# A fused attention, routing and expert kernel on one core: staged q and k halves written in place, narrow expert products, two output tiles begun together, more keep-warm matmuls

## The chip, the cores and the metric

One core of one Trainium2 chip runs the whole program. The metric is the device time of one execution in microseconds (us). Three executions before the change took 561.7, 564.54 and 566.77 us, median 564.54. The profiled execution, from which every row below comes, took 564.97 us, with a span of 563.3 us from its first to its last instruction.

## The reference, cut to what matters

```python
def _attn_ref(q, k, v, tau):            # 2 batches, 8 heads, 576 tokens, 64 per head
    scores = scale * np.matmul(q, k.transpose(0, 1, 3, 2))
    thresh = np.max(scores, axis=-1, keepdims=True) - tau
    scores = np.where(scores >= thresh, scores, -1000000000.0)
    ...softmax over the last axis...
    return np.matmul(attn, v)
def _moe_ref(x, w_gate, w1, w2, capacity):   # 1152 tokens, 512 wide, 8 experts, 1024 inside
    expert_idx = np.argmax(x @ w_gate, axis=1)
    ...each token to its one expert: out = gate * (relu(x @ w1[e]) @ w2[e])
def _moe2_ref(x, w_gate, w_val, w_out):      # 1536 inside, weights in float64
    g = x @ w_gate
    return (g / (1 + exp(-g)) * (x @ w_val)) @ w_out
```

The three run one after the other. Sums are kept near float32 precision: most operands are split in a high part rounded to the matmul's fp32r format and a low rest, and a product is made of hi*hi, hi*lo and lo*hi.

## The kernel before, in words

**Attention** (lines 308 to 963) takes the heads in four pairs (`hp` 0 to 3) and each pair in nine units (`st` 0 to 8): 128 query rows of one batch for both heads `j`, and as the ninth the 64 tail rows of both batches. A unit computes scores (`emit_qk`, L597: high and low part of q as stationary operand, one after the other, against `KP`, which holds k's high part in one half of the partitions and its low part in the other), the row maximum (L607), exp (L620), the mask (L631), the transposes of the previous unit (L653, copied out at L657), and some of a queue of other work: products with v (`pv_tasks`, L675 for the four main blocks of 128 keys, L678 for the 64 tail keys, where each head uses its own half of the partitions), the turning of the next pair's q and k, and the product with the router's weights (L709). The order on TensorE, VectorE (DVE), ScalarE (ACT) and GpSimd (POOL) is the order of the program text; SyncE (SP) issues nearly all DMAs, one after the other.

**Staging of the next pair** (`stage_tasks`, lines 493 to 574) is queued at unit `TST`, 4, and taken up from the next unit on, two tasks a unit; from unit `UST`, 5, these tasks go ahead of v products. A task turns 512 columns of k or q (`main`) or the tails of both, ACT copies the result, POOL writes the rounded part (L508) and the rest (L510) of all 128 partitions to a scratch tile, and SP copies from there by DMA to the places that `emit_qk` reads: 4 DMAs for each k main (L537), 4 for each q main (L540), 4 for k's tails (L559), and 8 for q's tails (L568, `qtails`, at unit `QST`, 1, of the pair itself). Per pair these are 28 DMAs. The order of tasks is k of batch 0, q of batch 0, tails, k of batch 1, q of batch 1. The first unit of the next pair needs the first three.

**Routing** (lines 966 to 1126) sorts tokens by expert in a chain of small DVE operations with a few matmuls between, with `keep_warm` matmuls on a zero tile (L775) behind three of its steps (`WA`). It ends in a branch on the load of the experts; the trace runs the branch `FAST`, in which the experts, sorted by load, have windows of 128, 128, 128, 144, 176, 192, 224 and 224 tokens. Behind the branch the first 128 gathered rows are scaled (L1181), turned (L1187), copied in two parts (L1193, L1194), and used by the first expert (L1267).

**Experts.** Those of width W above 128 go through `expert` (L1349). For each of 8 blocks `f` of the inner width, four partial products give `ps_h`; for each of 4 blocks `m` of the output, eight partial products over `f` give `ps_y`. A partial product (`mm_win`) is two matmuls: the weights' high part against both parts of the window side by side (2W columns, L1231), and their low part against the high part (W columns, L1232). `total` then adds the two halves: an ACT copy (L1240) and a DVE add (L1241). The relu is split by ACT (L1357) and DVE (L1358), one block behind. Between them the same two engines turn raw weights into pieces (L210, L288), and behind the first output block DVE cuts the next expert's window (`window`, L1226, L1227). `expert` issues output blocks one after the other, each followed by its way out to `yT` (L1240, L1241, L1405, L1406).

**The last layer** follows (L1447 on): TensorE products for gate and value, then for the output, with float64 weights converted by ACT and DVE meanwhile.

Of the kernel before, what the change touches and what calls it, by code (L numbers as in the profile page):

```python
# [10 lines left out]
F32 = mybir.dt.float32  # L11
# [11 lines left out]
def attention_moe_swiglu_kernel(  # L23
# [55 lines left out]
    WA = (4,9,12,0)  # L79
# [6 lines left out]
    TST = 4  # L86
    QST = 1
    FB = 1800
# [5 lines left out]
    UST = 5  # L94
# [222 lines left out]
    idw = ld.tile([128, KD, 128 + 2 * NE], F32, name="idw")  # L317

    def load_qkv(hp):
# [3 lines left out]
        for nm, (src, nb) in srcs.items():  # L323
            if hp and nm != "v":
                r[nm] = ld.tile([128, B, C4, 2, D], F32, tag=nm, name=nm, bufs=nb)
            else:
                r[nm] = ld.tile([128, B, 2, C4, D], F32, tag=nm, name=nm, bufs=nb)
            r[nm + "t"] = ld.tile([128, 2, D], F32, tag=nm + "t", name=nm + "t", bufs=nb)

        def main(nm, b, eng):  # L330
            if hp and nm != "v":
                for h in range(2):
                    eng.dma_start(r[nm][:, b, :, h],
                                  srcs[nm][0][b, h0 + h, 0:SM, :].rearrange("(p c) d -> p c d", c=C4))
# [4 lines left out]
        def tail(nm, eng):  # L339
            src = srcs[nm][0]  # L340
            for i in range(2):
# [6 lines left out]
                eng.dma_start(r[nm + "t"][i * ST:(i + 1) * ST], src_t)  # L348
# [7 lines left out]
        for b in range(B):  # L356
            main("v", b, nc.sync)
        tail("v", nc.sync)
# [42 lines left out]
    QT = [ld.tile([128, 2, 2 * 128], F32R, name=f"qt{j}") for j in range(2)]  # L401
    QTH, QTL = [[QT[j][:, w] for j in range(2)] for w in range(2)]
    traw = ld.tile([128, 2, 128], F32, name="traw")
    thl = ld.tile([128, 2, 2, 128], F32R, name="thl")
    qhl = [ld.tile([128, 2, B * SM], F32R, name=f"qhl{j}") for j in range(2)]
    ready = set()

    def tr_qk_tasks(hp):
# [6 lines left out]
        def ensure(j):  # L415
            if (hp, j) not in KP:
                KP[hp, j] = qk.tile([128, B, S], F32R, tag=f"kp{j}", name=f"kp{j}")
                QH[hp, j], QL[hp, j] = qhl[j][:, 0], qhl[j][:, 1]
                if hp % 2 == 0:
                    QH[hp, j], QL[hp, j] = ring[3 + j][:, 0], ring[3 + j][:, 1]  # L420
# [14 lines left out]
        def qmain(b, j, w):  # L435
            def f():
                ps = mp.tile([128, 512], F32R, tag="m", name="ps_q")
                tr(ps, [fl(raw[hp]["qh" if w == 0 else "ql"][:, b, j, c]) for c in range(C4)])
                dst = (QH, QL)[w][hp, j][:, b * SM:(b + 1) * SM]
# [53 lines left out]
    def stage_tasks(hp):  # L493
        kx, qx = ring[1], ring[0]
# [3 lines left out]
        def ensure():  # L498
            if (hp, 0) in KP:
                return  # L500
            for j in range(2):
                KP[hp, j] = qk.tile([128, B, S], F32R, tag=f"kp{j}", name=f"kp{j}")
                QH[hp, j], QL[hp, j] = qhl[j][:, 0], qhl[j][:, 1]
                if hp % 2 == 0:
                    QH[hp, j], QL[hp, j] = ring[3 + j][:, 0], ring[3 + j][:, 1]

        def parts(dst, src):
            nc.gpsimd.tensor_scalar(out=dst[0], in0=src, scalar1=1.0, scalar2=1.0,  # L508
                                    op0=ALU.mult, op1=ALU.mult)
            nc.gpsimd.tensor_tensor(out=dst[1], in0=src, in1=f32(dst[0]), op=ALU.subtract)  # L510
# [7 lines left out]
        def main(nm, b):  # L518
            def f():
# [4 lines left out]
                x, dst = (kx, sraw[:, 1, cs]) if nm == "k" else (qx, sraw[:, 0, cs])  # L524

                def ev():
# [19 lines left out]
        def tails():  # L546
# [3 lines left out]
            def ev():  # L550
# [3 lines left out]
                parts([thl[:, i] for i in range(2)], traw)  # L554
                for j in range(2):
                    o = 0 if j else SM
                    frm = slice(j * D, (j + 1) * D)
                    for i in range(2):
                        nc.sync.dma_start(  # L559
                            f32(KP[hp, j][i * D:(i + 1) * D, :, o:o + ST]),  # L560
# [996 lines left out]
```

## Time and profile before

| | |
|---|---|
| three executions | 561.7, 564.54, 566.77 us |
| profiled execution | 564.97 us, span 563.3 us |
| mean granted TensorE clock | 0.986 of full |
| attention, first score product to last | 9.8 to about 171 us |
| routing and branch | about 172 to 187 us |
| experts | 187 to 332 us |
| last layer | 332 to 559 us |

Read it by stretches: a share of busy time over the whole span mixes stages that wait for different things. In the rows below a time in front is the start in us from the span's beginning. A clock of 1.00 is 2.4 GHz and 0.50 is 1.2 GHz.

### The profile page before, as it was taken

To read this page: it belongs to the slowest core of one execution; us is meant where nothing else is said; L and a number is where in the kernel's file an instruction comes from. 1 tells how busy PE (TensorE), PEld (TensorE's weight loads), DVE (VectorE), ACT (ScalarE), POOL (GpSimd) and SP (SyncE) were. 2 spreads that over 40 slices of the span, in tenths; PEclk is the share of its full clock that TensorE was granted. 3 is DMA by queue.
4 is the path that set the end of the run, shared out by engine and by line. 5 is a ranking of instruction groups with operands and counts; after the bars stand their busy time and mean duration, and the time that the engine had idled before them with its cause. 6 is when DMAs were issued, how large, how long until landed. Compare 5 with 4: busy or idle time off the path is not lost. (4 is left out here: it accounts for less than half of the span.)

```text
span 563.3 us, 9844 instructions
## 1 busy us (share of the span) xinstructions
PE 536.4 (95%) x3600; PEld 481.0 (85%) x3602; DVE 409.7 (73%) x825; ACT 295.2 (52%) x573; POOL 85.4 (15%) x145
## 2 busy tenths in 40 slices
PE   7999988999997799999999999999999999999996
PEld 6787866877773799998998889999999999888884
DVE  5988876888876399989988977888896748722220
ACT  4977664676651399877866743334332333332321
POOL 6541050055452500000000000000000000011101
PEclk8999998999999799999999999999999999999999
DMA  7557467457301888977666442442341300000001
GB/s 185 173 150 171 118 143 172 110 140 205 116 29 35 313 289 281 328 224 232 224 219 223 151 149 81 145 149 83 143 149 76 112 40 1 0 38 37 20 38 42
DMA packets 67895, 77.94 MB, mean 138 GB/s; under 512 B 25216, under 2 KB 43136, under 8 KB 67840
## 3 DMA queue, kind: packets, MB, share of 16 engines
q1 hardware_dynamic: 66256, 72.52, 42.4%
q0 software_dynamic: 1440, 4.72, 2.2%
q8 instruction: 30, 0.49, 0.3%
q14 instruction: 25, 0.20, 0.1%
q10 hardware_dynamic: 144, 0.00, 0.0%
HBM read 61.89 MB, written 4.72 MB: 118 GB/s over the span
## 5 line engine op out<-in xcount | busy, mean ns | idle before, releaser
L1460 PE MATMUL pgv<-yT,ring 128*128 128x384 f32 x828 | 145.1, 337 | 0.0
L1460 PEld LDWEIGHTS pgv<-yT,ring 128*128 128x128 f32 x828 | 144.9, 188 | 0.0
L210 ACT CAST ring<-raw 128x1024 fp32r<-128x1024 f32 x57 | 60.8, 1066 | 51.2 <-DVE raw L238 49.5
L657 ACT COPY pT<-ps_pt 128x512 f32<-128x512 f32 (+1 forms) x108 | 52.3, 486 | 41.6 <-PE ps_pt L653 41.6
L607 DVE TENSOR_REDUCE nm<-s 128x1 f32<-128x576 f32 x72 | 54.4, 755 | 17.2 <-PE s L597 17.1
L631 DVE SCALAR_TENSOR_TENSOR e<-s,th,e 128x576 f32<-128x576 f32 x72 | 58.7, 816 | 6.2 <-ACT e L620 4.9
L1513 POOL DMA_INDIRECT out_dram<-ob,ids x9 | 8.7, 972 | 358.9 <-ACT ob L1512 351.7
L620 ACT ACTIVATE e<-s,nm 128x576 f32<-128x576 f32 x72 | 54.3, 754 | 2.2 <-DVE nm L607 1.8
L288 DVE TENSOR_TENSOR ring<-raw,ring 128x1024 fp32r<-128x1024 f32 x44 | 53.3, 1218 | 0.0
L1231 PE MATMUL ps_y<-h,ring 128*128 128x448 f32 (+3 forms) x160 | 48.8, 370 | 3.6 <-DVE h L1358 3.4
L214 DVE TENSOR_TENSOR hs<-h,hs 128x768 fp32r<-128x768 f32 x18 | 17.2, 958 | 48.1 <-ACT hs L210 48.1
L653 PE MATMUL ps_pt<-ident,e 128*128 128x128 f32 x324 | 47.9, 276 | 0.0
L1231 PE MATMUL ps_h<-xw,ring 128*128 128x448 f32 (+3 forms) x160 | 46.4, 362 | 0.0
L1508 PE MATMUL po<-ring,hs 128*128 128x512 f32 x108 | 42.0, 389 | 0.0
L1507 PE MATMUL po<-ring,hs 128*128 128x512 f32 x108 | 42.0, 389 | 0.0
L1509 PE MATMUL po<-ring,hs 128*128 128x512 f32 x108 | 42.0, 389 | 0.0
L1232 PE MATMUL ps_y<-h,ring 128*128 128x224 f32 (+3 forms) x160 | 40.0, 250 | 0.0
L1232 PE MATMUL ps_h<-xw,ring 128*128 128x224 f32 (+3 forms) x160 | 40.0, 250 | 0.0
L675 PE MATMUL ps_pv<-pT,v 128*64 128x256 f32 (+2 forms) x400 | 39.9, 331 | 0.0
L653 PEld LDWEIGHTS ps_pt<-ident,e 128*128 128x128 f32 x324 | 39.7, 142 | 0.2 <-issue 0.2
L1231 PEld LDWEIGHTS ps_y<-h,ring 128*128 128x128 f32 x160 | 30.0, 188 | 8.3 <-DVE h L1358 7.4
L1480 ACT ACTIVATE sg<-pgv 128x384 f32<-128x384 f32 x36 | 17.5, 486 | 28.4 <-PE pgv L1460 18.9
(224 smaller groups left out, 975.9 us busy)
## 6 DMA issues: line engine op xcount, KB each, us to landing
raw<-in_moe_w_dram SPq DMA_DIRECT2D x25, 1024.0 KB, 5.1
rawx<-in_moe_w_dram SPq DMA_DIRECT2D x7, 1024.0 KB, 5.9
raw<-in_moe_w_gate_dram SPq DMA_DIRECT2D x6, 1024.0 KB, 5.0
qhl<-ring SPq DMA_DIRECT2D x16, 256.0 KB, 4.4
raw<-in_moe_w_out_dram SPq DMA_DIRECT2D x4, 1024.0 KB, 4.9
kp<-ring SPq DMA_DIRECT2D x24, 128.0 KB, 2.3
rawx<-in_moe_w_val_dram SPq DMA_DIRECT2D x3, 1024.0 KB, 5.0
raw<-in_moe_w_val_dram SPq DMA_DIRECT2D x3, 1024.0 KB, 5.0
```

The source lines that it names most:

```text
L210: nc.scalar.copy(dst, src)
L288: lo_eng.tensor_tensor(out=lo_, in0=src, in1=f32(hi_), op=ALU.subtract)
L607: nc.vector.tensor_reduce(out=nm_t[u][:, j:j + 1], in_=s_t[i][:, :, 0:SH], axis=AX.XY, op=ALU.max, negate=True)
L620: nc.scalar.activation(out=e_t[u][:, j].rearrange("p (a s) -> p a s", a=2), in_=s_t[i][:, :, 0:SH], func=ACTF.Exp, bias=nm_t[u][:, j:j + 1 ...
L631: nc.vector.scalar_tensor_tensor(out=ev, in0=s_t.pop(i)[:, :, 0:SH], scalar=th_t[u][:, j:j + 1], in1=ev, op0=ALU.is_ge, op1=ALU.mult, accu ...
L653: nc.tensor.transpose(ps[:, c * 128:(c + 1) * 128], ef[:, (c0 + c) * 128:(c0 + c + 1) * 128], ident)
L657: return lambda: nc.scalar.copy(pT[g][:, c0:c0 + m, o:o + 128], ps[:, 0:m * 128].rearrange("p (c t) -> p c t", c=m))
L1231: mm(ps[:, 0:2 * W], ws(wp, 0), x[:, 0:2 * W], start=first, stop=False)
L1232: mm(ps[:, 0:W], ws(wp, 1), x[:, 0:W], start=False, stop=last)
L1460: mm(ps[:, 0:TH], (gw, vw)[w][:, i, kk, fl * 128:(fl + 1) * 128], yT[:, x, kk, th * TH:(th + 1) * TH], start=i + x + kk == 0, stop=i == 1 ...
L1507: mm(po, hs[:, 0, fl], ws[:, 0, sl], start=f == 0, stop=False)
L1508: mm(po, hs[:, 0, fl], ws[:, 1, sl], start=False, stop=False)
```

## The change

Attention. The four raw loads of q and k per pair become one DMA per tensor and batch. v's tail rows get a tile of their own per parity of the pair, zeroed once at the start by two DVE memsets; each head's 64 rows stand in its own half of the partitions with zeros in the other half, so that the tail product runs over all 128 partitions. Loads of v for pairs 2 and 3 move from unit 0 to unit 5 (`VST`). Staging is queued at unit 3 and goes first from unit 4. POOL now writes rounded part and rest separately for each half of the partitions, in place where the part already lies in the right half, and SP copies only the other half: 2 DMAs for each main, 2 for k's tails, 2 for q's tails (which POOL rounds in place first), 12 per pair in all. The tails come second in the order of tasks.

Routing and branch. Sixteen `keep_warm` matmuls of 512 columns follow the branch, four more follow the first transposes. A memset of the end of `xsT` moves from DVE to POOL. `late_consts` moves from unit 5 to unit 11. Nine small tiles share one buffer.

Experts. `mm_win` uses two matmuls up to 2W = 400, three of W columns above (the two experts of 224), and `total` then adds nothing. For the experts above 128, the first two output blocks are begun together: six partial products of block 0, six of block 1, then the last two of each.

```diff
-    WA = (4,9,12,0)
+    WA = (4,9,12,16,4)
-    TST = 4
+    TST = 3
+    VST = 5
-    UST = 5
+    UST = 4
...
+    vtail = [ld.tile([128, B, 2, D], F32, name=f"vtail{i}") for i in range(2)]
...
-                for h in range(2):
-                    eng.dma_start(r[nm][:, b, :, h], ...)
+                eng.dma_start(r[nm][:, b], ...)
...
-                eng.dma_start(r[nm + "t"][i * ST:(i + 1) * ST], src_t)
+                dst = r[nm + "t"][i * ST:(i + 1) * ST]
+                eng.dma_start(dst[:, :, i] if nm == "v" else dst, src_t)
...
+        if hp < 2:
+            values()
+        else:
+            vlate[hp] = values
...
-                    parts([x[:, i, cs] for i in range(2)], dst)
-                    for j in range(2):
-                        for i in range(2):
-                            to, frm = slice(i * D, (i + 1) * D), slice(j * D, (j + 1) * D)
-                            if nm == "k":
-                                o = ST if j else 0
-                                nc.sync.dma_start(f32(KP[hp, j][to, b, o:o + SM]), f32(x[frm, i, cs]))
-                            else:
-                                t = ring[3 + j] if hp % 2 == 0 else qhl[j]
-                                nc.sync.dma_start(f32(t[to, :, cs]), f32(x[frm, :, cs]))
+                    if nm == "k":
+                        k0, k1 = [KP[hp, j][:, b, o:o + SM] for j, o in ((0, 0), (1, ST))]
+                        x = kx[:, cs]
+                        rounded(k0[lo_], dst[lo_])
+                        rest_of(x[lo_], dst[lo_], k0[lo_])
+                        nc.sync.dma_start(f32(k0[up]), f32(x[lo_]))
+                        rounded(x[up], dst[up])
+                        rest_of(k1[up], dst[up], x[up])
+                        nc.sync.dma_start(f32(k1[lo_]), f32(x[up]))
+                    else:
+                        for j, frm, to in ((0, lo_, up), (1, up, lo_)):
+                            t = by_batch(ring[3 + j] if hp % 2 == 0 else qhl[j])[:, b]
+                            rounded(t[frm, 0:SM], dst[frm])
+                            rest_of(t[frm, SM:2 * SM], dst[frm], t[frm, 0:SM])
+                            nc.sync.dma_start(f32(t[to]), f32(t[frm]))
...
+                q4 = QT[j][:, :].rearrange("p (y t) -> p y t", t=ST)[:, 0:10:3]
+                x = thl[:, :, :].rearrange("p w (b t) -> p (w b) t", b=B)
+                rounded(q4[frm], f32(x[frm]))
+                nc.sync.dma_start(f32(q4[to]), f32(x[frm]))
...
-        return [main("k", 0), main("q", 0), tails, main("k", 1), main("q", 1)], qtails
+        return [main("k", 0), tails, main("q", 0), main("k", 1), main("q", 1)], qtails
...
-                        mm(ps[j * D:(j + 1) * D, o:o + w], r["vt"][j * ST:(j + 1) * ST, bb, :],
-                           p[j * ST:(j + 1) * ST, C4, o:o + w], start=False, stop=True)
+                        mm(ps[j * D:(j + 1) * D, o:o + w], r["vt"][:, bb, j, :],
+                           p[:, C4, o:o + w], start=False, stop=True)
...
-        for ev in [sort_tile(t) for t in range(NS0)]:
+        evs = [sort_tile(t) for t in range(NS0)]
+        keep_warm(ps8, WA[4])
+        for ev in evs:
             ev()
...
-        V.memset(xsT[:, :, NT:], 0.0)
+        nc.gpsimd.memset(xsT[:, :, NT:], 0.0)
...
-            if 2 * W <= 512:
+            if 2 * W <= 400:
...
-            if 2 * W > 512:
+            if 2 * W > 400:
                 return ps[:, 0:W]
...
+            head, tail_ = range(KF - 2), range(KF - 2, KF)
...
+                    if m == 0:
+                        products(0, head)
+                        products(1, head)
+                        products(0, tail_)
+                        products(1, tail_)
+                    elif m > 1:
+                        products(m, range(KF))
```

## Rows read from the trace of the kernel before

**Rows 1.** The page, part 1: busy us of each engine, share of the span.

```profile
PE 536.4 (95%) x3600; PEld 481.0 (85%) x3602; DVE 409.7 (73%) x825; ACT 295.2 (52%) x573; POOL 85.4 (15%) x145
```

**Rows 2.** Waits, whole span: who waited for whom, us in total, times, longest.

```profile
DVE nm L607 <- PE s L597: 17.1, 22, 3.3
...
PE ps_y L1231 <- DVE h L1358: 3.4, 5, 1.1
PE s L597 <- DMA kp<-thl: 3.4, 2, 3.1
```

**Rows 3.** Windows: stretch, us, busy PE, PEld, DVE, ACT, POOL, clock, DMA share, GB/s.

```profile
86.50:89.90 3.40, 3.40 (x17) 2.97 (x17) 2.31 (x4) 1.71 (x4) 0.00 (x0) 0.50 0.55 136
...
185.50:192.30 6.80, 5.99 (x28) 5.59 (x27) 2.83 (x6) 2.22 (x3) 5.25 (x6) 0.50 1.02 396
```

**Rows 4.** Timeline of SP's queue, 60 to 90 us: start, us, issues merged.

```profile
62.58 6.15 SPq L568 DMA_DIRECT2D qt<-thl  x8
...
70.72 3.11 SPq L537 DMA_DIRECT2D kp<-ring  x4
...
79.73 3.23 SPq L559 DMA_DIRECT2D kp<-thl  x4
```

**Rows 5.** Timeline of POOL, 58 to 92 us: start, us.

```profile
72.01 0.61 POOL L508 TENSOR_SCALAR ring<-raw 128x512 fp32r<-128x512 f32 x1
72.71 1.29 POOL L510 TENSOR_TENSOR ring<-raw,ring 128x512 fp32r<-128x512 f32 x1
```

**Rows 6.** Groups by line: busy us, mean ns.

```profile
L678 PE MATMUL ps_pv<-pT,vt 64*64 64x256 f32 (+2 forms) x100 | 13.3, 342 | 0.0
```

**Rows 7.** Timelines of PE, main and tail products with v, 48 to 53 us.

```profile
48.01 0.39 PE L675 MATMUL ps_pv<-pT,v 128*64 128x256 f32 x2
48.32 0.43 PE L678 MATMUL ps_pv<-pT,vt 64*64 64x256 f32 x2
...
48.59 0.38 PE L678 MATMUL ps_pv<-pT,vt 64*64 64x256 f32 x2
...
51.15 1.95 PE L675 MATMUL ps_pv<-pT,v 128*64 128x256 f32 x16
```

**Rows 8.** Timeline of PE, 178 to 198 us, around the branch.

```profile
179.37 2.75 PE L775 MATMUL ps_w<-dummy 128*128 128x512 bf16 x11
185.39 1.02 PE L1187 MATMUL ps_g<-ident,raw 128*128 128x128 f32 x4 [3.26 <-DVE raw L1181]
187.21 5.38 PE L1267 MATMUL ps_h<-ring,xw 128*128 128x256 f32 x24 [0.81 <-issue]
...
194.88 1.68 PE L1267 MATMUL ps_h<-ring,xw 128*128 128x256 f32 x12
```

**Rows 9.** Windows, columns as in rows 3: inner and output stretches of three experts.

```profile
249.81:258.57 8.76, 8.76 (x66) 8.76 (x65) 7.83 (x17) 6.95 (x17) 0.00 (x0) 1.00 0.66 210
258.57:269.13 10.56, 9.45 (x67) 8.82 (x65) 9.55 (x20) 7.00 (x16) 0.00 (x0) 1.00 0.74 252
...
298.77:309.68 10.91, 10.78 (x66) 9.56 (x65) 9.54 (x17) 6.84 (x15) 0.00 (x0) 1.00 0.68 226
309.68:319.71 10.03, 10.03 (x66) 9.57 (x65) 9.42 (x18) 8.46 (x19) 0.00 (x0) 1.00 0.66 212
319.71:332.02 12.31, 11.29 (x66) 9.56 (x65) 11.16 (x24) 5.76 (x14) 0.00 (x0) 1.00 0.27 83
```

**Rows 10.** Timeline of weight loads (PEld) in an expert of 224.

```profile
306.14 0.19 PEld L1231 LDWEIGHTS ps_y<-h,ring 128*128 128x128 f32 x1
306.25 0.19 PEld L1232 LDWEIGHTS ps_y<-h,ring 128*128 128x128 f32 x1
306.45 0.19 PEld L1231 LDWEIGHTS ps_y<-h,ring 128*128 128x128 f32 x1
```

**Rows 11.** Timelines of PE and of DVE, output stretch of the expert of 176.

```profile
261.22 0.43 PE L1231 MATMUL ps_y<-h,ring 128*128 128x352 f32 x1 [1.11 <-DVE h L1358]
...
263.22 0.33 DVE L1241 TENSOR_TENSOR a<-a,ps_y 128x176 f32<-128x176 f32 x1
```

More of the change, by code (lines that the diff above doesn't have):

```diff
@@ L355, in load_qkv, with values @@
         tail("q", nc.sync)
-        for b in range(B):
-            main("v", b, nc.sync)
-        tail("v", nc.sync)
+        def values():
+            for b in range(B):
+                main("v", b, nc.sync)
+            tail("v", nc.sync)
+        if hp < 2:
+            values()
+        else:
+            vlate[hp] = values
+    vlate = {}
     def prep_tasks(hp, pick):
@@ L400, in attention_moe_swiglu_kernel, with by_batch, q_pair @@
     QH, QL, KP = {}, {}, {}
-    QT = [ld.tile([128, 2, 2 * 128], F32R, name=f"qt{j}") for j in range(2)]
-    QTH, QTL = [[QT[j][:, w] for j in range(2)] for w in range(2)]
+    QT = [ld.tile([128, 5 * 128], F32R, name=f"qt{j}") for j in range(2)]
+    QTH, QTL = [[QT[j][:, w * 384:w * 384 + 256] for j in range(2)] for w in range(2)]
     traw = ld.tile([128, 2, 128], F32, name="traw")
-    thl = ld.tile([128, 2, 2, 128], F32R, name="thl")
+    thl = ld.tile([128, 2, 128], F32R, name="thl")
+    kth = ld.tile([128, 128], F32R, name="kth")
     qhl = [ld.tile([128, 2, B * SM], F32R, name=f"qhl{j}") for j in range(2)]
     ready = set()
+    def by_batch(t):
+        return t[:, :, :].rearrange("p w n -> p (w n)").rearrange("p (b n) -> p b n", b=B)
+    def q_pair(hp, j):
+        t = by_batch(ring[3 + j] if hp % 2 == 0 else qhl[j])
+        return [t[:, :, w * SM:(w + 1) * SM] for w in range(2)]
     def tr_qk_tasks(hp):
@@ L417, in ensure @@
                 KP[hp, j] = qk.tile([128, B, S], F32R, tag=f"kp{j}", name=f"kp{j}")
-                QH[hp, j], QL[hp, j] = qhl[j][:, 0], qhl[j][:, 1]
-                if hp % 2 == 0:
-                    QH[hp, j], QL[hp, j] = ring[3 + j][:, 0], ring[3 + j][:, 1]
+                QH[hp, j], QL[hp, j] = q_pair(hp, j)
         def kmain(b, j):
@@ L493, in stage_tasks @@
     def stage_tasks(hp):
-        kx, qx = ring[1], ring[0]
+        kx = ring[1][:, 0]
         sraw = raw_buf[2][:, :].rearrange("p (i n) -> p i n", i=2)
@@ L502, in ensure, with rounded, rest_of @@
                 KP[hp, j] = qk.tile([128, B, S], F32R, tag=f"kp{j}", name=f"kp{j}")
[L503 to L508, printed above, removed]
+                QH[hp, j], QL[hp, j] = q_pair(hp, j)
+        def rounded(dst, src):
+            nc.gpsimd.tensor_scalar(out=dst, in0=src, scalar1=1.0, scalar2=1.0,
                                     op0=ALU.mult, op1=ALU.mult)
-            nc.gpsimd.tensor_tensor(out=dst[1], in0=src, in1=f32(dst[0]), op=ALU.subtract)
+        def rest_of(dst, src, hi):
+            nc.gpsimd.tensor_tensor(out=dst, in0=src, in1=f32(hi), op=ALU.subtract)
         def turn(blocks, name):
@@ L523, in f @@
                 cs = slice(b * SM, (b + 1) * SM)
-                x, dst = (kx, sraw[:, 1, cs]) if nm == "k" else (qx, sraw[:, 0, cs])
+                dst = sraw[:, 1 if nm == "k" else 0, cs]
                 def ev():
@@ L778, in attention_moe_swiglu_kernel @@
     keep_warm(mp, WARM0, 128)
+    for vz in vtail:
+        nc.vector.memset(vz, 0.0)
     nc.scalar.dma_start(tau_sb, tau.partition_broadcast(128))
@@ L938, in attention_moe_swiglu_kernel @@
             qtails()
+        if live and st == VST and hp + 1 in vlate:
+            assert not any(g[0] < hp for _, _, g in pvq)
+            vlate.pop(hp + 1)()
     assert not trq
@@ L1386, in expert, with products @@
                         next_piece()
+            pys = {}
+            def products(m, fs):
+                if fs[0] == 0:
+                    ps = ps8.tile([128, 512], F32, tag="m", name="ps_y")
+                    pys[m] = ps, pieces.pop(("w2", e, m))[:, :, :].rearrange(
+                        "p i (k f) -> p i k f", k=KF)
+                ps, wv = pys[m]
+                for f in fs:
+                    mm_win(W, ps, wv, lambda w, i: w[:, i, f], hs[f], f == 0, f == KF - 1)
+            head, tail_ = range(KF - 2), range(KF - 2, KF)
             for m in range(KD):
-                ps = ps8.tile([128, 512], F32, tag="m", name="ps_y")
                 if e in halves:
+                    ps = ps8.tile([128, 512], F32, tag="m", name="ps_y")
                     for f in range(KF):
@@ L1395, in expert @@
                 else:
-                    wp = pieces.pop(("w2", e, m))
-                    wv = wp[:, :, :].rearrange("p i (k f) -> p i k f", k=KF)
-                    for f in range(KF):
-                        mm_win(W, ps, wv, lambda w, i: w[:, i, f], hs[f], f == 0, f == KF - 1)
+                    if m == 0:
[5 more added lines that the diff above has]
+                        products(m, range(KF))
+                    ps = pys[m][0]
                 if e == 0:
```

50 lines of the change are left out of this document (27 added, 23 removed).

## The prediction

> **What bounds the kernel now.** The first part of the page [rows 1] gives TensorE 95% busy, so only TensorE's own time counts: what its work takes, the gaps in it, and the stretches in which its clock is half. The view of waits [rows 2] gives the gaps by releaser, the windows [rows 3] the two long stretches at 0.50 that end a gap, and the timelines and windows of stretches [rows 4 to 11] the price of each step. DVE is 73% busy over the span, which hides that it sets the pace in single stretches: 9.55 of 10.56 us in one output stretch [rows 9]. The sum is made against the profiled execution, 564.97 us; the median of the runs is 0.43 us lower. One per cent, 5.6 us, is about what a measurement of this kernel can tell from no change.
>
> **Staging of q and k.** Now: TensorE waits for k's tails (`kp<-thl`) 3.4 us in two places, 3.1 of it before the second pair [rows 2], and runs the 3.40 us behind that at 0.50 [rows 3], which costs half of them, 1.7 us. The wait's last link is SP's queue: SP works through 28 issues per pair one by one, 6.15/8 = 0.77 us each for `qtails`, 3.11/4 = 0.78 for a k main, 3.23/4 = 0.81 for k's tails, and these last four end at 79.73 + 3.23 = 82.96 us [rows 4], with the landing behind that. After: 12 issues, some 9.5 us instead of 22, and half the bytes; the tails stand second, not third, and the tasks start a unit earlier (about 4 us). The raw loads' halves merge, which takes two issues per tensor and batch to one; moving v's loads of the later pairs to unit 5 puts at most some 8 issues (6.3 us) into SP's queue among the staged copies, but behind the tails' and k's copies of batch 0 and, at the worst, ahead of q's. The added price is POOL's: a main takes 0.61 + 1.29 = 1.9 us on 128 partitions [rows 5]; on 64 partitions an instruction takes at least half of that (sum 1.9, nothing lost) and, if only the columns count, as much (3.8 us). I take the upper end, since the two instructions move the same 512 columns. The chain on POOL before the next pair's first unit is then k 3.8, tails some 2.3 (by the same rows, with 128 columns for four instructions of each kind: (0.61 + 1.29) × 128/512 × 4 = 1.9, and starts), q 3.8, together 9.9 us. Begun one unit earlier than the 72.01 us of now, less the tasks that stand ahead, at about 66, it ends near 76; two issues and a landing later, near 81, q stands ready, against 82.5 when TensorE comes. The slack of 1.5 us is small, and a later boundary has the same. So the wait vanishes: −3.4 − 1.7 = **−5.1**; bounds 0 (a new wait of the same size) and −5.1. `qtails` gets POOL work of a quarter of a main at unit 1 and is needed at unit 8: hidden. The memsets of v's tail tiles lie on DVE in the start, ahead of the first scores, where the engines wait for loads; without that cover, two instructions of some 0.3 us. The memset moved to POOL (15% busy) and `late_consts` at unit 11: nothing, as both have tens of us until the first reader.
>
> **v's tail products.** 100 of them, now 64*64 [rows 6]. Two main products in a row start 1.95 − 0.39 = 1.56 us over seven steps of pairs apart, 0.22 per pair; from a main to a tail pair it is 48.32 − 48.01 = 0.31, and from the first tail pair to the next 0.27 [rows 7]. So a change of shape costs (0.31 + 0.27 − 2 × 0.22) = 0.14 us. With 128 rows there is none. The trace has 19 changes into the tail form and 12 back into the main form: 31 × 0.14 = 4.3 us. Attention is at TensorE's pace in the last three pairs (DVE waits for scores 17.1 us in 22 places [rows 2]) and at DVE's in the first, whose share I drop, and a little more for units that end with a DVE wait: **−3.0**, bounds 0 and −4.3.
>
> Against this stands a rule. The trace: a tail product takes as long per column as a main one (0.38 a pair against 0.39 [rows 7]), so halved rows win nothing now, and the sum goes by that. The Trainium skill, "TensorEngine Tiling (Array Packing)", sections "When to Use Tiling" and "Theoretical Speedup", asks for 2× row tiling where the contracted dimension is 64 or less, and promises up to 2×. By it the two heads' tail products would be running side by side now, and the change would take that from them: 50 pairs × 0.22 = 11 us at most where all were overlapped, and half of it, 5.5, for the half of them that is a full pair. It is a rival below.
>
> **The branch.** Now TensorE's last keep-warm matmuls end at 182.1, it waits 3.26 us for the gathered rows (L1181) and has 0.50 from 185.50 to 192.30 [rows 3, 8]. The 24 products of L1267 take 5.38 us there; twelve take 1.68 at full clock, so 24 take 3.36. Gain 2.0, and a further 0.5 from the four transposes (1.02 us) [rows 8]. Sixteen matmuls at 2.75/11 = 0.25 us, or 0.21 by their 512 columns, are 3.4 to 4.0 us from about 182: they end at 185.4 to 186.0, against transposes that could start at 185.39, so they delay these by 0 to 0.6. The four after the transposes take 0.85 to 1.0 us, in the 0.81 us that TensorE is idle there. Together −2.0 − 0.5 + 0.3 = **−2.2**, bounds −2.6 and +0.5: the second if expert 0 is held by something else (its raw weights, ACT's and DVE's split), as the DMA share of 1.02 in the stretch [rows 3] makes possible.
>
> **The experts.** Narrow products: a pair (448 + 224 columns) takes 0.31 us, its loads 0.11 and 0.20 apart [rows 10]. Three products of 224 have loads at best 0.11 apart, as the row's closest, so 0.33: 0.02 × 64 products × 2 experts = **+2.6**; bounds 0, and +5 if each of the three costs 0.01 more. In return `total` drops 12 ACT copies and DVE adds of the two experts, 0.33 us each on DVE [rows 11].
> The two blocks: output stretches are longer than inner ones by 10.56 − 8.76 = 1.8 us (176), 10.91 against the other stretch's 10.03, 0.9 (224), and 12.31 − 10.03 = 2.3 (224) [rows 9]; the experts of 144 and 192, not shown, I put at 1.5 and 1.0 from the 0.9 and 0.5 us that lie between. The wait stands ahead of the sixth product, 1.11 us [rows 11], and has f = 5, which is in `head`: it stays. What the new order covers is the wait for f = 6 and 7, about 0.5 us an expert. On the other side block 0 ends six pairs later, 6 × 0.27 − 0.5 = 1.1 us; its add on DVE (L1241, 263.22 us [rows 11]), which stands in order ahead of the next expert's window and of its weights' pieces, goes with it, on an engine busy 9.55 of 10.56 us [rows 9]. So in the experts of 144 to 192 the delay is carried on, about +1.3 by their end, while in the two of 224 DVE has 12 × 0.33 = 4.0 us less to do, and their 0.9 + 2.3 vanish. Sum: +1.3 + 2.6 − 3.2 = **+0.7**; bounds −5 (no narrow cost, all output waits gone) and +4 (no wait gone).
>
> **The sum.** −5.1 − 3.0 − 2.2 + 0.7 = −9.6: 564.97 − 9.6 = 555.4, in terms of the median 555.0.
>
> **The rivals.**
> (a) *The two blocks hide all output waits*: 1.8 + 0.9 + 2.3 + 1.5 + 1.0 = 7.5 us instead of the share above, so −3.2 + 2.6 becomes −7.5 + 2.6 and the delay falls away: 5.6 lower, 549.4. For it: six more products stand between the last relu and its reader. Against it: the wait is ahead of the sixth. 0.12.
> (b) *The branch gives nothing*: the keep-warm matmuls delay the transposes or the first expert waits for its weights. 2.2 to 2.7 back, 557.5. For it: DMA share 1.02; against: TensorE is busy 5.99 of 6.80 us at half clock [rows 3]. 0.13.
> (c) *Attention gains half*: POOL's chain leaves part of the wait or DVE sets the pace of the pairs. 8.1/2 back, 559. 0.14.
> (d) *Row tiling is lost*: tails 5.5 slower instead of 3.0 faster, 563.5. Against: the equal time per pair. 0.05.
> (e) *Slower: POOL's chain is late.* Its place: the boundary before each of the three staged pairs, TensorE's first score products waiting for `q`'s copy. The slack is 1.5 us, so it decides from a chain of 11.4 us instead of 9.9, which instructions on 64 partitions 1.15 times as long as on 128 would make; at 1.5 times it is 14.7 us, three waits of 14.7 − 11.4 = 3.3 with 1.7 of half clock each, 15 us in all, which is 555 + 15 = 570 and so the point from which the change as a whole is slower by 1%; at 1.7 times 576. For it: the doubled instructions; against: nothing in [rows 5] suggests more than equal time, and SP's queue is freed. 0.04.
> The forecast itself keeps 0.52, with 552 to 558 from its own bounds.
>
> **Range and chances.** From 548.5, (a) and a little, to 561.5, (c) with narrow products at their upper bound; outside lie (d), (e) and tails of the others. Faster by over 1% is below 558.9: the forecast, (a), most of (b) and a fraction of (c): 0.76. Same: the rest of (b) and (c), and (d): 0.20. Slower: (e), 0.04.
>
> **What would show it.** Staging right: no wait on `kp`, 12 SP issues per pair, no stretch at 0.50 behind 86 us; wrong: a wait of L597 on `qt`, `ring` or `qhl`. Tails right: L678 as 128*64, changes gone, 0.22 a pair. Branch right: a clock near 1.00 from 185.5 on and L1267's first 24 near 3.4 us; wrong: the same end of expert 0. Experts right: loads 0.11 apart three in a row, 24 fewer adds (L1241), a larger wait ahead of a sixth product in the experts of 144 to 192, and output stretches of 224 near 10.7. The prediction is wrong above all if the output waits all vanish, or if the pairs' boundaries get a new wait.

## The result, and the profile after

Twelve executions of the changed kernel have a median of 559.72 us (558.06 to 562.36), twelve of the kernel before 565.13 us: ratio 0.990, 95% interval 0.9879 to 0.9922, 5.4 us less. The forecast was 555.0, within 548.5 to 561.5. The profiled execution took 560.4 us with a span of 558.7 us, against 564.97 and 563.3 before, so 4.6 us less in span. Where these 4.6 us lie, from the start times in the two traces (us):

| stretch | before | after | difference |
|---|---|---|---|
| start to the first index matmul (L1095, now L1129) | 178.43 | 169.96 | −8.47 |
| from there to the first output product of the expert of 144 | 62.05 | 63.87 | +1.82 |
| from there to the first product of the last layer | 91.54 | 94.74 | +3.20 |
| last layer to the end | 231.28 | 230.13 | −1.15 |

The page, part 1, busy us of each engine after (before: [rows 1]), and three rows of its waits (who waited for whom, us in total, times, longest):

```profile
PE 536.2 (96%) x3750; PEld 488.6 (87%) x3750; DVE 403.3 (72%) x802; ACT 287.7 (51%) x549; POOL 115.3 (21%) x188
```

```profile
DVE nm L634 <- PE s L624: 8.2, 15, 1.3
...
PE ps_y L1267 <- DVE h L1394: 3.9, 4, 1.1
PE ps_ht L1313 <- ACT hb L1323: 3.2, 2, 2.6
```

The wait of TensorE for `kp<-thl` [rows 2] has gone. A new one has come, `ps_ht` for `hb`, and the one of the output stretches (`ps_y` for `h`) is not smaller: 3.9 us, where [rows 2] had 3.4. POOL works 30 us more, and no wait of TensorE for staged q or k shows for it.

**The boundary.** The old wait, from TensorE's timeline before the change:

```profile
86.14 0.57 PE L597 MATMUL s<-kp,ring 128*128 128x288 f32 x2 [3.06 <-DMA kp<-thl]
```

After: timeline of POOL, of SP's queue, and the window at the same boundary (columns as in rows 3):

```profile
65.43 0.61 POOL L526 TENSOR_SCALAR kp<-raw 64x512 fp32r<-64x512 f32 x1 [3.55 <-ACT raw L548]
66.13 1.27 POOL L530 TENSOR_TENSOR ring<-raw,kp 64x512 fp32r<-64x512 f32 x1
...
75.15 1.28 POOL L530 TENSOR_TENSOR ring<-raw,ring 64x512 fp32r<-64x512 f32 x1
```

```profile
74.39 2.54 SPq L566 DMA_DIRECT2D ring<-ring  x2
```

```profile
82.50:87.50 5.00, 5.00 (x43) 4.01 (x42) 4.73 (x13) 2.88 (x6) 3.03 (x6) 1.00 0.55 118
```

An instruction of POOL on 64 partitions takes as long as one on 128 [rows 5]. The chain k, tails, q runs from 65.43 to 76.43, q's last copy is issued at 76.93 and lands 4.1 us after its issue began, near 80.5; TensorE begins the scores that read it at 83.5 and goes through the boundary without a gap at full clock.

**The branch.** Timelines of TensorE and ACT, then the window behind, columns as before:

```profile
171.09 6.48 PE L802 MATMUL ps_w<-dummy 128*128 128x512 bf16 x28
177.41 0.60 PE L1221 MATMUL ps_g<-ident,raw 128*128 128x128 f32 x4
177.85 1.03 PE L802 MATMUL ps_w<-dummy 128*128 128x512 bf16 x4
178.84 3.13 PE L1303 MATMUL ps_h<-ring,xw 128*128 128x256 f32 x24
...
182.17 1.68 PE L1303 MATMUL ps_h<-ring,xw 128*128 128x256 f32 x12
186.47 1.11 PE L1313 MATMUL ps_ht<-ident,hb 128*128 128x128 f32 x4 [2.63 <-ACT hb L1323]
```

```profile
184.88 1.04 ACT L211 CAST ring<-raw 128x1024 fp32r<-128x1024 f32 x1 [4.75 <-PE ps_h L1303]
185.83 0.59 ACT L1323 ACTIVATE hb<-ps_h 128x512 f32<-128x512 f32 x1
```

```profile
186.40:189.70 3.30, 3.23 (x15) 3.23 (x16) 2.12 (x3) 2.87 (x5) 0.00 (x0) 0.50 0.33 131
```

The first 24 products take 3.13 us where they took 5.38 [rows 8]. Then ACT's conversion, which waits for the first twelve of them, starts at 184.88, though by their records they end near 180.5. The relu stands behind it on ACT, TensorE waits 2.63 us for the relu, and half clock follows. Saved and given back: 185.39 to 192.42, 7.03 us, has become 177.41 to 181.81, 4.40 us; the next 4.35 us of work (192.42 to 196.76 before) take 8.44 (181.81 to 190.25).

**The experts.** Windows, columns as in rows 3: inner and output stretch of 176, output stretch of 192, both stretches of the second expert of 224.

```profile
242.59:251.34 8.75, 8.75 (x67) 8.75 (x65) 7.56 (x16) 6.95 (x17) 0.00 (x0) 1.00 0.66 235
251.34:265.61 14.27, 12.25 (x66) 11.62 (x65) 10.05 (x21) 7.75 (x18) 0.00 (x0) 0.76 0.55 171
...
274.90:285.68 10.78, 9.64 (x66) 9.15 (x65) 8.74 (x18) 6.10 (x16) 0.00 (x0) 1.00 0.60 194
...
307.14:317.86 10.72, 10.72 (x99) 10.72 (x97) 9.74 (x18) 6.63 (x13) 0.00 (x0) 1.00 0.65 223
317.86:328.57 10.71, 10.71 (x98) 10.71 (x97) 7.00 (x12) 3.49 (x7) 0.00 (x0) 1.00 0.24 75
```

Timelines of TensorE in the output stretch of 176, and of weight loads in an expert of 224:

```profile
253.22 0.43 PE L1267 MATMUL ps_y<-h,ring 128*128 128x352 f32 x1 [0.89 <-DVE h L1394]
...
255.36 0.66 PE L1267 MATMUL ps_y<-h,ring 128*128 128x352 f32 x1 [1.12 <-DVE h L1394]
```

```profile
297.99 0.19 PEld L1232 LDWEIGHTS ps_y<-h,ring 128*128 128x128 f32 x1
298.10 0.19 PEld L1233 LDWEIGHTS ps_y<-h,ring 128*128 128x128 f32 x1
298.21 0.19 PEld L1234 LDWEIGHTS ps_y<-h,ring 128*128 128x128 f32 x1
```

In the expert of 176 TensorE waits ahead of the fourth and of the sixth product, where before there was one wait [rows 11], and the clock is at half from 254.6 us, inside the second wait, to 261.5: 0.76 over the stretch, 14.27 us instead of 10.56 [rows 9]. The experts of 224 have no wait left, and each stretch is as long as its loads, 0.11 us apart.

### The profile page after: what moved, and what is told of

Read it like the earlier page. It is cut to its first block, busy times and chain, and to the rows that moved or that the text cites. A ratio compares the mean times of both kernels' runs of the same rounds, so it can differ in the third digit from the quotient of the medians.

```text
span 558.7 us, 10058 instructions
## 1 busy us (share of the span) xinstructions
PE 536.2 (96%) x3750; PEld 488.6 (87%) x3750; DVE 403.3 (72%) x802; ACT 287.7 (51%) x549; POOL 115.3 (21%) x188
## 5 line engine op out<-in xcount | busy, mean ns | idle before, releaser
L1267 PE MATMUL ps_y<-h,ring 128*128 128x288 f32 (+2 forms) x96 | 29.7, 383 | 3.9 <-DVE h L1394 3.9
L1533 DVE TENSOR_TENSOR h<-sg,pgv 128x384 f32<-128x384 f32 x36 | 19.7, 549 | 17.6 <-PE pgv L1512 17.2
L211 ACT CAST ring<-rawx 128x1024 fp32r<-128x1024 f32 x19 | 20.1, 1067 | 21.6 <-DVE rawx L239 21.5
L702 PEld LDWEIGHTS ps_pv<-pT,v 128*64 128x64 f32 x400 | 21.6, 136 | 10.7 <-issue 4.2
L624 PE MATMUL s<-kp,ring 128*128 128x288 f32 x128 | 25.4, 318 | 2.1 <-DVE th L642 1.1
```

Of the source, the lines that this page charges most:

```text
L211: nc.scalar.copy(dst, src)
L702: mm(ps[j * D:(j + 1) * D, o:o + w], r["v"][:, bb, j, c, :], p[:, j * (C4 + 1) + c, o:o + w], start=c == 0, stop=False)
```

## The experiments

Kernels of one group ran on one chip; the groups are on different chips, so ratios to the kernel before of the same group are compared. That does not take the chip out altogether: the kernel with the output blocks in order has 0.9803 on one chip and 0.9873 on another, 4 us apart. The first group has no unaltered changed kernel, so its medians are set against the 0.990 of another chip and are uncertain by that much; its traces are compared with each other where possible.

**First group.** *Tails on 64 rows again:*

```diff
-mm(ps[...], r["vt"][:, bb, j, :], p[:, C4, o:o + w], ...)
+mm(ps[...], r["vt"][j*ST:(j+1)*ST, bb, j, :], p[j*ST:(j+1)*ST, C4, o:o + w], ...)
```

> The changed kernel with v's tail products again on 64 partitions a head (the tile of zeros stays). The changed kernel's attention ends 8.3 us earlier than before; 5.0 of that lie at the boundary before the third pair, the rest in the last two pairs. Theory: the rest is the price of changing the tile shape, 0.14 us a change: the end of attention comes 2.5 to 4.3 us later than in the changed kernel (163.6 us), the whole about 562.7 us, and main products are again followed by a tail pair after 0.31 us instead of 0.22. Rival: the rest comes from the staging (fewer stalls behind DVE), and tails on 64 rows cost at most 0.7: about 560.

Measured: 561.89 us, ratio 0.9961 (0.9936 to 0.9985). The index matmuls start at 174.61 us, against 170.25 in the kernel with the same attention but for this (in order, below): 4.4 us. By the medians, across chips, it is 0.9961 − 0.990 of 564 us, 3.4. Timelines of TensorE, first of the changed kernel, then of this one, the same three groups of products:

```profile
38.34 0.65 PE L702 MATMUL ps_pv<-pT,v 128*64 128x256 f32 x4
38.82 0.60 PE L705 MATMUL ps_pv<-pT,vtail 128*64 128x256 f32 x4
39.26 1.03 PE L702 MATMUL ps_pv<-pT,v 128*64 128x256 f32 x8
```

```profile
38.60 0.65 PE L702 MATMUL ps_pv<-pT,v 128*64 128x256 f32 x4
39.18 0.65 PE L705 MATMUL ps_pv<-pT,vtail 64*64 64x256 f32 x4
39.76 1.08 PE L702 MATMUL ps_pv<-pT,v 128*64 128x256 f32 x8
```

From start to start 0.48 + 0.44 against 0.58 + 0.58: two changes of shape cost 0.24 us. The theory holds, with its upper end of 4.3 just passed in the trace; the rival falls.

*No added keep-warm matmuls:* 

```diff
-    WA = (4,9,12,16,4)
+    WA = (4,9,12,0,0)
```

> The changed kernel without the sixteen keep-warm matmuls at the branch and the four behind the first transposes. In the changed kernel they save 2.6 us in the first 24 expert products, and then TensorE waits 2.6 us for ScalarE in the first expert and runs 3.4 us at half clock. Theory: the first expert is held by what arrives late while the DMA engines are saturated, so the saved time is only waited for: without the matmuls the first products are slow again, the wait of 2.6 us and the half clock behind it go, and the expert of 144 starts within 1 us of the changed kernel's 225.7: total 559 to 561. Rival: the wait has nothing to do with the keep-warm matmuls and stays: the expert of 144 starts 2 to 2.6 us later, total about 562.

Measured: 559.17 us, ratio 0.9912 (0.988 to 0.9945), as the changed kernel on another chip. From the index matmuls to the first output product of 144: 61.4 us (233.45 − 172.03). The wait of 2.6 us is gone and the first products are slow again, as the theory had it. But it is absent in the three others of this group too, which have the matmuls and take 61.1 to 61.3: the wait isn't their doing alone. Over the whole stretch the matmuls save 0.3 us or less on this chip. But the gathered rows happened to be there early in this execution: DVE first scales them 6.66 us after the index matmuls' start, against 7.96 to 8.68 in the other three. From that moment on the stretch takes 54.8 us here and 52.6 to 53.2 with the matmuls, so behind the rows they save 1.6 to 2.2 us in these traces.

*Output blocks one after the other:*

```diff
-products(0, head); products(1, head); products(0, tail_); products(1, tail_)
+products(m, range(KF))
```

> The changed kernel with the output blocks of the wide experts issued one after the other again (narrow products stay). Theory: the order of two blocks moves block 0's adds 1 us later in DVE's queue and so makes the next expert's relu late: in the changed kernel's trace the output stretch of the expert of 176 has two waits of 0.9 and 1.1 us and 6.8 us at half clock behind them. With the old order the stretch goes from 14.3 us back to about 10.6, the one of 144 from 8.8 to 9.3, those of 224 stay at 10.7 to 11.2 since they have no adds: total 1.5 to 3 us less than the changed kernel, about 557.5. Rival: the order is what hides the output waits of the experts of 224, and without it 0.9 and 2.3 us come back there: total about 560.

Measured: 553.96 us, ratio 0.9803 (0.9779 to 0.9827), 5.5 us less than the changed kernel across chips, more than the theory's 1.5 to 3 us; repeated below on another chip. The stretch of 176 takes 12.15 us in this execution, again with 3.4 us at half clock, and not the 10.6 of the theory (10.55 in the repetition). The experts of 224 keep 10.72 us a stretch, so the order is not what hides their waits: the rival falls.

*Two wide matmuls and an add for 224:*

```diff
-            if 2 * W <= 400:
+            if 2 * W <= 512:
```

> The changed kernel with the two experts of 224 computed by two wide matmuls a product and an add, as before; the new order of blocks stays. In the changed kernel each of their four stretches takes 10.72 us, against 10.03 for an undisturbed stretch of before. Theory: narrow products cost 0.69 us a stretch, 2.8 in all, and what they buy is DVE and ScalarE time, which ends the output waits of 0.9 and 2.3 us: without them the stretches of the inner width go back to 10.0 and the output stretches to 11 to 12.5: total within 1 us of the changed kernel. Rival: the order of blocks alone hides these waits: all four stretches take 10.0, total 2.8 us less, about 557.

Measured: 565.46 us, ratio 1.0006 (0.9983 to 1.0029): 6 us more than the changed kernel across chips, against theory and rival. Windows, columns as before: output stretch of the first expert of 224, both stretches of the second, start of the last layer; then two waits of TensorE's timeline:

```profile
292.96:305.05 12.09, 10.81 (x66) 9.56 (x65) 9.68 (x19) 7.01 (x17) 0.00 (x0) 1.00 0.61 192
305.05:315.08 10.03, 10.03 (x67) 9.57 (x65) 9.14 (x18) 7.87 (x17) 0.00 (x0) 1.00 0.68 222
315.08:330.93 15.85, 13.81 (x67) 12.03 (x65) 11.72 (x24) 6.49 (x17) 0.00 (x0) 0.78 0.20 62
330.93:340.00 9.07, 7.47 (x31) 6.62 (x30) 6.59 (x12) 3.19 (x7) 0.00 (x0) 0.81 0.51 198
```

```profile
318.05 0.48 PE L1267 MATMUL ps_y<-h,ring 128*128 128x448 f32 x1 [1.76 <-DVE h L1394]
333.71 2.57 PE L1523 MATMUL pgv<-yT,ring 128*128 128x384 f32 x10 [1.59 <-ACT yT L1457]
```

The inner stretch goes from 10.72 to 10.03, but with the adds on DVE the output stretches are longer than before the change (10.91 and 12.31 [rows 9]), with half clock behind, and the delay reaches the last layer. On the same chip the kernel with tails on 64 rows, whose code for the experts is that of the changed kernel, takes 92.69 us from the first output product of 144 to the last layer and 230.11 us from there to the end; this one takes 99.40 and 234.08, so 10.7 us more, of which 1.5 lie in the expert of 176, whose code is the same (3.4 us at half clock there). So with two blocks begun together the narrow products are worth more than they cost. Wide products with the blocks in order were not run on the changed kernel.

**Second group.** *The changed kernel unaltered:*

> The changed kernel itself, unaltered, as the measure for the others of this group and as a second profiled execution. Its first one had TensorE waiting 2.6 us in the first expert with 3.4 us of half clock behind, and 6.8 us of half clock in the output stretch of the expert of 176. Theory: both come and go between executions, since four kernels with the same code up to there (three of them) or with fewer keep-warm matmuls show no such wait in the first expert: it is absent here, the experts' part from the index matmuls to the last layer takes 154 us instead of 158.6, and the total is 558 to 560.5. Rival: both belong to this order of the program and come again: 158 to 159 us.

Measured: 561.72 us, ratio 0.991 (0.9889 to 0.9931). The first expert's wait is there again, 2.61 us; the half clock in the expert of 176 is not (11.45 us instead of 14.27). So the theory was wrong on the first and right on the second. The part from the index matmuls to the last layer takes 158.1 us, as the rival had it, and not 154.

*Staging one unit later:*

```diff
-    TST = 3
+    TST = 4
-    UST = 4
+    UST = 5
```

> The changed kernel with staging queued one unit later, as before (taken up from unit 5, not 4); the halves are still written in place with 12 DMAs a pair. Theory: the old wait came from SP's 28 issues, not from the time at which the tasks were queued; POOL's chain (k 3.8, tails 2.6, q 3.8 us) ends about 4 us later, near 80.5, and q lands near 83 to 84, so the boundary before the third pair has a wait of 0 to 1.5 us; total within 2 us of the changed kernel. Rival: the earlier unit is what removes the wait: 3 us of wait and 3.4 us of half clock come back at each boundary, 5 us or more in all, about 564.

Measured: 562.88 us, ratio 0.9929 (0.9911 to 0.9946), 1.2 us more than the group's changed kernel. Timeline of TensorE, its waits over 0.6 us between 44 and 140 us:

```profile
46.25 0.78 PE L624 MATMUL s<-kp,qhl 128*128 128x288 f32 x4 [0.74 <-DMA qhl<-qhl]
82.90 0.77 PE L624 MATMUL s<-kp,ring 128*128 128x288 f32 x4 [0.64 <-DVE rinv L724]
121.76 0.77 PE L624 MATMUL s<-kp,qhl 128*128 128x288 f32 x4 [0.67 <-DVE nm L634]
138.07 0.76 PE L624 MATMUL s<-kp,qhl 128*128 128x288 f32 x4 [1.33 <-issue]
```

The first three lines are the boundaries: 0.6 to 0.7 us each, as the theory had it. Each ends 0.1 to 0.3 us after a copy of q has landed (46.11, 82.65 and 121.56 us), also where the profile names DVE. The fourth is none of a boundary. So the new copies removed the old wait and the earlier unit only this rest. Fewer DMAs and the tails' place in the order are both in this kernel; which of the two was needed is not shown.

*POOL's subtractions twice:*

```diff
 rest_of(x[lo_], dst[lo_], k0[lo_])
+rest_of(x[lo_], dst[lo_], k0[lo_])
...
```

> The changed kernel with POOL's subtraction for each main half done twice (same operands, same result), 1.27 us more for each half, so 5.1 us more on POOL's chain before the next pair's first unit. Theory: in the changed kernel the last half of q is issued at 76.9 us and TensorE asks for it at about 82.5, so the slack with a landing of 3 us is 2.5 to 3 us, and 2 to 2.6 us of wait appear at each of three boundaries, with half clock behind some of them: total 5 to 12 us more, 565 to 571. Rival (the prediction's slack of 1.5 us): 3.6 us a boundary and half clock behind each, 16 us more, 575. Second rival: the scheduling of other work around the boundary hides it, within 2 us.

Measured: 573.66 us, ratio 1.0125 (1.0105 to 1.0145), 11.9 us more than the group's changed kernel. Timeline of TensorE, its waits over 1 us between 40 and 135 us:

```profile
48.46 1.03 PE L627 MATMUL s<-kp,qhl 128*128 128x288 f32 x4 [1.78 <-DMA qhl<-qhl]
63.58 1.30 PE L627 MATMUL s<-kp,qhl 128*128 128x288 f32 x4 [3.94 <-DVE th L645]
94.54 0.77 PE L627 MATMUL s<-kp,ring 128*128 128x288 f32 x4 [1.18 <-DVE xr L767]
133.84 0.77 PE L627 MATMUL s<-kp,qhl 128*128 128x288 f32 x4 [1.56 <-DMA qhl<-qhl]
```

5.1 us more on the chain give 1.2 to 1.8 us of wait at each boundary, so the slack is about 3.5 us. All three are waits for q: its last copy lands at 48.33, 94.34 and 133.59 us, just before they end (the profile puts the second down to `xr`). They are shorter than the theory's 2 to 2.6 us, and half clock follows the first alone (3.4 us). That the total lies at the upper end of the theory's 5 to 12 us is luck: the wait of 3.94 us is none of a boundary, and 6.8 us at half clock come with it, together 7.3 us of the 12.9 by which the index matmuls start later than in the group's changed kernel (183.06 against 170.15). DVE waits 2.96 us there for a constant (`tok`) that `late_consts` puts into POOL's queue behind the staging.

*In order and without the added keep-warm matmuls* (both edits above):

> The kernel with the output blocks one after the other (553.96 us) without the twenty added keep-warm matmuls. That kernel's runs scatter by 2.3 us only, so the matmuls' worth shows better here. Theory: they save 2.1 us behind the transposes (half clock over the first products) and lose part of it, since at times they end later than the gathered rows arrive: 1 to 2 us more without them, about 555.5. Rival: worth nothing, within 0.7 us.

Measured: 558.15 us, ratio 0.9846 (0.9825 to 0.9867), on another chip than the kernel in order (0.9803). What the matmuls are worth can't be read from two chips that differ in the first expert's wait, so this one is inconclusive. Beside the changed kernel of its own chip it is 3.6 us faster, where the order alone gives 1.8 on the third chip (below): no sign that the matmuls pay.

**Third group.** *The changed kernel and the kernel in order side by side:*

> The changed kernel unaltered, again beside the others of this group, since its first repetition and the kernel with the old block order ran on different chips. Theory: ratio 0.990 to 0.991 to the kernel before. On the chip of the first repetition the first expert had its wait of 2.6 us, on the other not one of three kernels with the same code up to there: here it is there or not together with the two other kernels of this group that keep this code.

> The kernel with the output blocks one after the other again (553.96 us beside 564.23 us of the kernel before, on another chip). Theory: the order of blocks costs what the traces show, 1.6 us of waits in the experts of 176 and 192 less 0.5 in the one of 144, and one more half clock of 3.4 us in part of the executions: 2 to 4 us less than the changed kernel beside it. Rival: the whole 5.6 us of the two ratios, 0.9803 against 0.9900, belongs to the order: 5 to 6 us less.

Measured: 560.53 us, ratio 0.9911 (0.9882 to 0.994), and 558.71 us, ratio 0.9873 (0.9845 to 0.99). Windows of the output stretches of 176 and 192, first with two blocks begun together, then in order:

```profile
252.16:263.63 11.47, 9.45 (x66) 8.81 (x65) 9.45 (x19) 7.14 (x18) 0.00 (x0) 1.00 0.62 193
272.92:284.34 11.42, 9.86 (x66) 9.15 (x65) 9.37 (x18) 6.73 (x18) 0.00 (x0) 1.00 0.61 196
```

```profile
253.96:264.51 10.55, 9.43 (x67) 8.80 (x65) 9.54 (x20) 7.00 (x16) 0.00 (x0) 1.00 0.73 250
273.80:284.26 10.46, 9.99 (x67) 9.30 (x65) 9.43 (x18) 6.71 (x14) 0.00 (x0) 1.00 0.74 243
```

At full clock the order costs 0.92 + 0.96 us there and gives 0.76 in the expert of 144 (9.34 to 8.58): 1.1 us net, 1.8 by the medians. The direction agrees with the theory, just below its 2 to 4; the two intervals overlap, so the medians alone do not show it. The rival's 5 to 6 us fall: the larger step of the first group contains the first expert's wait, which that chip did not have. Beginning two blocks together is thus a part of the change that gains nothing in these runs.

*GpSimd adds the output halves* (in order, 144 to 192):

```diff
-a = total(W, ps)
+nc.scalar.copy(a, ps[:, W:2 * W]); nc.scalar.copy(a1, ps[:, 0:W])
+nc.gpsimd.tensor_tensor(out=a, in0=a, in1=a1, op=ALU.add)
```

> The kernel with the output blocks in order, in which ScalarE copies both halves of an output block of the experts of 144 to 192 and GpSimd adds them: DVE loses four adds of 0.33 us an expert. Theory: DVE's chain sets these output stretches (1.1 us of wait in the expert of 176, 0.46 in the one of 192), so four adds less in the expert before end the waits of the next: 1 to 2 us less than in order alone, about 1.5. Rival: GpSimd's adds slow DVE's own instructions or come so late that the exit of a block holds the next: same or 1 to 2 us slower.

Measured: 559.25 us, ratio 0.9895 (0.9866 to 0.9923), no faster than in order alone. The wait in the expert of 176 is 1.13 us as before, and the one in the expert of 192 grew from 0.47 to 0.92: four adds of the expert before are not what makes the relu late.

*Twenty small matmuls at the start* (in order):

```diff
     keep_warm(mp, WARM0, 128)
+    keep_warm(mp, 20, 8)
```

> The kernel with the output blocks in order and twenty small matmuls of 8 columns more at the start, beside the keep-warm ones there (0.3 us or nothing in time): every later matmul stands 40 instructions further on in TensorE's code. Theory: the wait of the first expert (ScalarE's conversion starts 4.3 us after the matmuls that it waits for have ended by their records) comes with TensorE's own code load, which lands 0.2 us before it starts, in a stretch where the DMA engines are full: shifted by 40 instructions the load falls elsewhere and the wait is gone or at another place. Rival: the wait depends on the chip and not on the place in the code: present here exactly if it is present in the kernel in order beside it.

Measured: 558.14 us, ratio 0.9867 (0.984 to 0.9894), as in order. TensorE's code load, one packet of the instruction queue, moved from 185.89 to 181.51 us; the wait in the first expert was 1.18 us instead of the 2.09 of the kernel in order beside it. Timeline of ACT of this kernel:

```profile
186.56 1.04 ACT L211 CAST ring<-raw 128x1024 fp32r<-128x1024 f32 x1 [4.29 <-PE ps_h L1304]
```

ACT's conversion still waits for products that by their records ended long before, now 5 us after the code load instead of 1.1. So the code load's place doesn't explain it. The wait (1.1 to 2.7 us) is in all eight profiles outside the first group that have the keep-warm matmuls, and in none of the first group's three: it goes with the chip, as the rival has it, but only one chip is without it, and what differs there is not shown.

## Why the prediction was right, and where its sum was not

The measured 559.72 us lie in the stated range, which is 13 us wide; of the 9.6 us that the sum promised, 5.4 came. Whether the change gains more than 1%, to which the prediction gave 0.76, is not decided: the interval of the ratio is 0.9879 to 0.9922. One of the three parts came as forecast, one did not, one came with the right mechanism and too low a price; the last layer, which the sum did not have, made up 1.15 us by luck.

**Staging and tails, right.** Predicted −5.1 and −3.0; the start of the index matmuls moved by 8.47 us. The old wait of 3.06 us, at 86.14, lies before the third pair and not before the second, as the prediction has it; that changes nothing in its sum. This boundary, from the row maximum of the second pair's ninth unit to that of the third pair's second, went from 13.69 us (78.86 to 92.55) to 8.70, so 5.0. The choice of the upper end for POOL's 64 partitions was exact (0.61 and 1.27 us), the chain took 11.0 us instead of 9.9, and the slack was about 3.5, not 1.5 us: q's last copy stands ready near 80.5, close to the forecast 81, but the scores that read it begin at 83.5 and not at 82.5. Rival (e) was further off than it seemed. The tails cost 3.4 to 4.4 us on 64 rows, at the upper bound of 4.3.

**The rule on row tiling.** The trace shows a change of shape that costs 0.12 us and halved rows that win nothing. The Trainium skill ("TensorEngine Tiling (Array Packing)", "When to Use Tiling") asks for row tiling at a contracted dimension of 64; here the measurement decides against it, with 3.4 to 4.4 us the other way. Rival (d) falls.

**The branch, wrong.** The step that failed is "Together −2.0 − 0.5 + 0.3 = −2.2". Its first half is right: 7.03 us became 4.40. That the saved time would go through the first expert is not: the next stretch gave back 4.1 us (a wait of 2.63 us and the 3.41 us at half clock that follow) in this profile, and the whole stretch became 1.82 us longer, outside the bound of +0.5. One profile of the kernel before stands behind the 62.05 us; the other ten with the matmuls take 61.1 to 65.5, so the 2.2 us came in none of them. Where the wait was missing (first group) the matmuls did save 1.6 to 2.2 us behind the rows. Rival (b) came about, by a wait that it had not named: ACT's conversion and the relu behind it, not the first expert's weights. The gathered rows came no earlier either: DVE first scales them 6.5 us after the index matmuls' start here, 6.9 to 10.4 in the other ten profiles with the matmuls, 6.7 and 11.1 in the two without, 6.2 before. That is not TensorE's doing: POOL's first gather starts 0.9 us (before) and 1.2 to 1.3 us (all others) after the last write of `xd` has landed, and that landing comes 1.5 us after the index matmuls' start before the change and here, 1.6 to 3.1 in the other profiles.

**The experts, right on the mechanism, wrong on its price.** The delay of the sixth relu carried on from expert to expert, as the prediction has it: at full clock the stretch from the first output product of 144 to the last layer takes 92.65 us (second group) against 91.54, +1.1 where +0.7 was forecast, narrow products included (4 × 0.69 = 2.8 against 2.6) and both waits of 224 gone (3.2). What the sum lacked is the clock: with two waits 2.1 us apart in the expert of 176 come 6.8 us at half clock in the profiled execution, 2.8 us more than in the second group's. It comes in part of the executions only. And the narrow products were worth more than the sum gave them: without them the kernel is 6 us slower by the medians across chips, 10.7 by two traces of one chip, in the output stretches and the start of the last layer. A gain that the sum had not is the last layer, 1.15 us: its first 36 products took 7.48 us (332.02 to 339.50) with 1.4 us of pauses behind `yT` on ACT and DVE, and take 6.33 now. It goes with the narrow products: from its first product to the end, every kernel that has them takes 230.1 to 230.3 us.

**The difference of the sum**, 9.6 − 4.6 = 5.0 us: 4.0 at the branch, 2.5 in the experts, less 0.4 in attention and 1.15 in the last layer.

**Open:** why ACT's wait on TensorE ends 3 to 4 us after the products that it names, on some chips. It lies in a stretch in which the DMA engines are full (share 1.04 from 180 to 185 us), but so they are in the first group's kernel in order (1.03 from 182 to 186), which has no such wait. The place of TensorE's code load does not settle it either. A weaker form stands already in the trace before the change, where the 24 products end at 192.59 [rows 8] and the relu behind them starts 1.2 us later, with ACT idle:

```profile
193.82 0.60 ACT L1287 ACTIVATE hb<-ps_h 128x512 f32<-128x512 f32 x1 [2.60 <-PE ps_h L1267]
```

## What to carry to other kernels

Time saved in front of a stage is not saved until the first chain behind it (here conversion, relu, transposes) has been followed instruction by instruction on each engine. An order that fills one wait moves a late engine's work later, and in a chain of equal stages the next one pays; here only the two experts whose adds were taken from that engine came out without a wait. A gain that is read from one profile of each kernel can be as small as what changes from one chip to the next (here 4 us in one stretch): run the kernels to be compared on one chip. A wait has two prices: its length, and the half clock that may follow.

## What was not expected of the hardware

With TensorE waits as short as 0.9 and 1.1 us, 1.0 us of work apart, came 6.8 us at 1.2 GHz in one execution (254.6 to 261.5 us), and 3.4 us or none in kernels with the same code in the experts. Keep-warm matmuls themselves ran at half clock for 3.4 us (from 171.1 us) in the second group's profile of the changed kernel, with no wait of their own ahead but the 1.57 and 1.40 us of the routing chain; behind the same two waits the first profile of this kernel stays at 2.4 GHz. POOL's instructions take the same time on 64 partitions as on 128 (0.61 and 1.27 to 1.28 us against 0.61 and 1.29).
